# Five of the row turns of a two-layer SSM and MLP step as DMA transposes, with loads, stores and norms rearranged

## The chip, the cores and the metric

The kernel runs on one core of a Trainium2 chip. The metric is the device time of one execution in microseconds (us). Inside a core, TensorE (PE) multiplies matrices, VectorE (DVE), ScalarE (ACT) and GpSimd (POOL) work on elements, and SyncE (SP) only issues DMA transfers; ACT and POOL can issue DMAs too. Each engine runs its own instructions strictly in order, and semaphores join them.

## The reference, cut to what matters

Two kinds of layer alternate twice, on a sequence of 2048 rows with 448 channels, in bf16. The program returns the output and, for a given gradient of the output, the gradients of all nine inputs but `B_x`, which is not used.

```python
def A(q, k, v, shift_k, ssm_k, ssm_D):          # long convolution
    kv = sum(pad(k, 3)[:, t:t+S] * shift_k[:, 3-t] for t in range(4)) * v
    y  = irfft(rfft(pad(kv)) * rfft(pad(ssm_k)))[:S]      # length 2*S
    return q * (y + kv * ssm_D)
def B(x, w1, w2):                               # 448 -> 1792 -> 448
    return silu(x @ w1) @ w2
x = A_q
x = x + A(layernorm(x), ...);  x = x + B(layernorm(x), w1, w2)
x = x + A(layernorm(x), ...);  x = x + B(layernorm(x), w1, w2)
# out = x; and the vector-Jacobian product with grad_out
```

Since k, v and the convolution weights do not depend on x, the convolved rows Y are computed once and serve both A layers.

## The kernel before

The kernel has three stages.

**The prefix** (to about 105 us) transforms the convolution weights and kv with matrix-multiply FFTs and leaves Y in SBUF. At its end the first rows are normalised.

**The main loop**, `Main.run` (L777 and on), goes over four chunks c of 512 rows. A matmul contracts over the partitions, so the normalised rows, which lie with rows on partitions, have to be turned before w1 can be applied: `nT` holds them with channels on partitions, as four blocks of 128 channels (the last two overlap) by 512 rows. The steps are generators, and a hand-written string says in what order PE runs them (`weave`): one letter is one step.

- H is `h = nT x w1` (seven steps of 8 products, L510), with silu on ACT and a transposed store of the activation, `aT`.
- O is the product with w2 (L692, eight steps of 7 matmuls), whose result DVE adds to the rows X.
- G is the gradient through w2 (L510, seven steps), N the gradient through w1 (L738, eight steps of 7 matmuls) with the backward pass of the norms on DVE.
- T is a turn: `transp` (L570 to 578) makes eight 128x128 PE transposes into a PSUM bank, which ACT copies to `nT`; a turn has two such steps, so 16 transposes and two copies.
- J is a step of `Jobs`, the weight gradients, whose blocks are read back from HBM. They start in the last chunk and run on into the suffix.

In chunk c the order on PE is: O of layer 1 (with G for the next stretch and, for the chunks 1 and 2, the turn of the next chunk's `n01` rows among its last steps), N of layer 1 woven with H(c+1, 0), O of layer 0, G, and N of layer 0 woven with H(c+1, 1), between whose first steps the `n1` rows of chunk c+1 are turned. H(c+1, 0) and H(c+1, 1) wait for the turned rows, and every step of H needs all 512 rows.

SP's queue is in order too. `store` (L563 to 569) writes each half of an activation or gradient to HBM turned: two DMA transposes SBUF to SBUF (16 and 12 blocks of 128x128) into "turned" buffers, of which there are two, and two plain stores, each behind its transpose's landing. `load_gT` (L762, L763) brings a chunk of grad_out turned from DRAM, as eight DMA transposes of three blocks or one. The `nT` tiles and gT share two buffers.

PE's order is that of the program text. The order on the other engines' queues is made by a planner from its own estimates of when each instruction is due; `issue_after` binds one instruction behind another.

**The suffix**, `_ssm_suffix`, turns the gradient of Y into those of k, v and the convolution weights by FFTs and inverse FFTs, with Jobs woven between. `Jobs.load` (L965 to 981) fetches one block of 512 KB on SP; `load_n3`, `n1` and `go2` fetch the other operands. `spec_load` reads the spectra of the prefix back on POOL. `fin_w2` and `fin_w1` copy results out; `flush` turns w1's. The last seven w2 blocks (f = 7 to 13) come at the very end.

`_ln_steps` (L255 to 281) normalises: batch statistics on DVE, the power on POOL, one DVE instruction for `-mean*rstd` (`ln_nmr`, L273), and one for `x*rstd + nmr` (L278).

Of the kernel before, what the change touches and what calls it, by code (L numbers as in the profile page):

```python
# [10 lines left out]
FP32 = mybir.dt.float32  # L11
BF16 = mybir.dt.bfloat16
ACT = mybir.ActivationFunctionType
ALU = mybir.AluOpType
# [3 lines left out]
P = 128  # L18
S = 2048
D = 448  # L20
# [87 lines left out]

def _copy(nc, eng, out, in_):
    if eng is nc.scalar:  # L110
        nc.scalar.copy(out, in_)
    else:
        eng.tensor_copy(out, in_)


class K:
# [86 lines left out]
def _fft_stage1(k, n2, rhs, A1, psum, m=None, eng=None):  # L203
    nc = k.nc
    ps = psum.tile([P, 2, 512], FP32, name="ps_s1", **k.pt["s1"])
    for c in range(2):
        nc.tensor.matmul(ps[:, c, :D], lhsT=k.M1sb[:, n2 if m is None else m, c, :], rhs=rhs, start=True, stop=True)  # L207
    _copy(nc, eng or nc.scalar, A1[:, :, :, n2, :].rearrange("p dh c ds -> p c dh ds"), ps[:, :, :D].rearrange("p c (dh ds) -> p c dh ds", ds=4))


def _fft_stage2(k, Zt, psum, consume, chunks=range(NCI)):
# [41 lines left out]
def _ln_steps(k, pool, c, src, si, n_g, groups=((0, 4),), pin=False, eng=None, behind=None, store=()):  # L253
    nc = k.nc
    for lo, hi in groups:  # L255
        n = hi - lo
        st = pool.tile([P, 4, 6], FP32, name="ln_st", tag="ln_st", bufs=1)
        mv = pool.tile([P, 4, 2], FP32, name="ln_mv", tag="ln_mv", bufs=2)
        for tl in range(lo, hi):
            with ExitStack() as es:  # L260
                if behind:
                    es.enter_context(k.tc.issue_after(behind[tl].ins))
                i = nc.vector.bn_stats(out=st[:, tl, :], in_=src(tl))
            if pin:
# [7 lines left out]
        nmr = pool.tile([P, 4], FP32, name="ln_nmr", tag="ln_nmr", bufs=2)  # L272
        nc.vector.scalar_tensor_tensor(out=nmr[:, lo:hi], in0=mv[:, lo:hi, 0], scalar=-1.0, in1=r[:, lo:hi], op0=ALU.mult, op1=ALU.mult)  # L273
        for tl in range(lo, hi):
            if eng is nc.scalar:
                nc.scalar.activation(n_g[:, tl, :], src(tl), ACT.Identity, bias=nmr[:, tl:tl + 1], scale=r[:, tl:tl + 1])
            else:
                k.ln_last = nc.vector.tensor_scalar(out=n_g[:, tl, :], in0=src(tl), scalar1=r[:, tl:tl + 1], scalar2=nmr[:, tl:tl + 1], op0=ALU.mult, op1=ALU.add)  # L278
# [256 lines left out]
class Main:  # L535
# [221 lines left out]
    def load_gT(self, c, gT):  # L757
        nc = self.nc
        src = _pm(self.k.grad_out[0])
        for tl in range(4):  # L760
            ts = slice(tl * P, (tl + 1) * P)
            nc.sync.dma_start_transpose(out=gT[:, 0:3, ts], in_=src[:, 4 * c + tl, 0:384])  # L762
            nc.sync.dma_start_transpose(out=gT[:, 3:4, ts], in_=src[:, 4 * c + tl, 320:448])  # L763

    def T(self, src, dst):
        for h in range(2):
            self.transp(src, dst, h)
            yield
# [12 lines left out]
    def run(self, es):  # L781
# [52 lines left out]
        for c in range(4):  # L834
# [7 lines left out]
            steps("OOOO", O=o)  # L842
            if c < 3:
                self.fwd0b(c + 1)
            if c == 0:
                weave("O" * 4, O=o)
            else:
                if c == 1:
                    gh2, g = gh21, g21
                else:  # L850
                    gh2 = []
                    g = self.G(gT, gh2)
                if c == 1:
# [18 lines left out]
            if c < 3:  # L872
                r = []
                if c == 0:
                    weave("NTNTNHNNHHNNHHNHH", N=n, T=self.T(self.n0[1][1], nT), H=self.H(c + 1, 0, nT, r, (10, 11)))
                else:
                    weave("NHNNHHNNHHNNHHN", N=n, H=self.H(c + 1, 0, nT, r))
                gb = gb_load(c + 1)
                aT, dT1 = r
                weave("OOOOOOTOTO", O=self.O(c + 1, 0, aT), T=tg)  # L880
                self.fwd1(c + 1, [self.chain] * 4)
                g = self.G(gT, gh1, dT0)
                if c:
                    gT = self.nT()
                    self.load_gT(c + 1, gT)
                    weave("G" * 7, G=g)
                else:
                    weave("G" * 7, G=g)
# [30 lines left out]
class Jobs:  # L919
# [48 lines left out]
    def load(self, key, ft):  # L968
        k, nc = self.k, self.nc
        i = self.n_ld  # L970
        self.n_ld += 1
        if self.pool is None and i % 2 and i > 3:
            st = _hd(k, [P, NT, P], "dstat")
        else:
            st = k.dp3.tile([P, NT, P], BF16, name="dstat", tag="dstat", bufs=3)
        src = k.OP_d[key]
        with ExitStack() as es:
            if self.last_ld is not None:
                es.enter_context(k.tc.issue_after(self.last_ld.ins))
            self.last_ld = nc.sync.dma_start(out=st[:], in_=src[:, ft, :, :])  # L980
        return st
# [46 lines left out]
    def steps(self):  # L1028
# [39 lines left out]
    def fin_w2(self, ft, ps):  # L1068
        nc, k = self.nc, self.k
        o = self.out()  # L1070
        if ft == NF - 1:
            nc.scalar.copy(o[:, 0:256], ps[:, 0:256])
            nc.vector.tensor_copy(o[:, 256:D], ps[:, 256:D])
        else:
            nc.scalar.copy(o[:], ps[:, :D])
# [59 lines left out]
def _ssm_suffix(k):  # L1135
# [9 lines left out]
    with ExitStack() as es:  # L1145
# [6 lines left out]
        B1k = A1[:].rearrange("p a c n s -> p (a c n s)").rearrange("p (q d) -> p q d", d=D)  # L1152
        for n2 in range(16):
            k.M1sb = k.m1h[n2 // 8]
            _fft_stage1(k, n2, gY[:, n2, :], A1, psum, n2 % 8)
            jobs.run(1)
        with ExitStack() as e1:
            p1 = e1.enter_context(tc.tile_pool(name="sspec2", bufs=1, reuse_waits="tile"))
# [7 lines left out]
            def spec_load(cp):  # L1166
                lo, hi = cp * 2048, (cp + 1) * 2048
                kk = (kk0 if cp == 0 else kk1 if cp == 1 else sp.tile([P, 2, 2048], BF16, name="kk_c", tag="kk0") if cp % 2 == 0
                      else p1.tile([P, 2, 2048], BF16, name="kk_d", tag="kk1"))
                nc.gpsimd.dma_start(out=kk[:, 0, :], in_=k.SPEC_d["K"][:, lo:hi])  # L1170
                i = nc.gpsimd.dma_start(out=kk[:, 1, :], in_=k.SPEC_d["KV"][:, lo:hi])
                if cp == 2:
                    with tc.issue_after(i.ins):
                        _load_minv(k, nc.gpsimd)
                return kk

            kks = [spec_load(0)]
            for g in range(7):
                pt = psum.tile([P, 16, P], BF16, name="ps_tr", **mm)
                for i in range(16):  # L1180
                    nc.tensor.transpose(pt[:, i, :], A1f[:, 16 * g + i, :], k.ident[:])  # L1181
                if g % 2:
                    nc.scalar.copy(Zf[g], pt[:].rearrange("p a b -> p (a b)"))
# [83 lines left out]
        for dc in range(ND):  # L1267
            gK = p2.tile([DC, S], BF16, name="gK", tag="gK", bufs=3)
            gKv = gK[:].rearrange("p (n1 n2) -> p n1 n2", n2=16)
            for g in range(2):  # L1270
# [82 lines left out]
```

## Time and profile before

| | us |
|---|---|
| median of three runs | 727.19 |
| the three runs | 723.72, 729.2, 727.19 |
| the profiled execution | 728.88 |
| its span, first to last instruction | 727.1 |
| PE busy | 693.8 (95%) |
| DVE busy | 490.2 (67%) |
| ACT busy | 441.3 (61%) |
| POOL busy | 124.9 (17%) |
| SP queue's DMAs (q1), share of 16 DMA engines | 61.5% |
| mean TensorE clock granted | 0.990 |

The main loop takes about 103 to 503 us of the span, 92 us a chunk. In views of the trace, a line names the engine, the source line, the operation and its tiles (`out<-in`), and after a bar or in brackets the idle time ahead of it with what ended it. A timeline line starts with start and duration in us; `x8` means that eight equal neighbours are joined. `SPq` is SP's queue of DMA issues: the duration is that of the issue, not of the transfer. PEclk is the clock granted to TensorE, 1.00 being full speed. A DMA landing is counted from its issue.

### The profile page before, as it was taken

How to read it: one execution, taken by the hardware profiler on the slowest of the kernel's cores; microseconds unless marked ns; L12 is line 12 of the kernel's file. 1: busy time of each engine (PE TensorE's matmuls, PEld its weight loads, DVE VectorE, ACT ScalarE, POOL GpSimd, SP SyncE). 2: the span in 40 equal slices, each digit the busy share in tenths (PEclk: the TensorE clock that was granted, in tenths of full speed). 3: DMA queues.
4: the chain of work that ended last, by engine and by line, in shares of the span. 5: the costliest groups of instructions: out<-in, count | busy, mean ns of one | idle time of the engine just before them, and what ended most of it. 6: DMA issues, size and time to landing. Idle time of an engine off the chain costs nothing.

```text
span 727.1 us, 12759 instructions
## 1 busy us (share of the span) xinstructions
PE 693.8 (95%) x4976; PEld 379.6 (52%) x4976; DVE 490.2 (67%) x1150; ACT 441.3 (61%) x577; POOL 124.9 (17%) x213
## 2 busy tenths in 40 slices
PE   6998989899999999999999999999699999999898
PEld 4876644334444444444444444545366666656554
DVE  5789866668886758975488525635058778859780
ACT  4877978585877869587786783224555555454200
POOL 1134310101020100111002000001112233243230
PEclk9999999999999999999999999999989999999999
DMA  9949997569978999599885995299997798689871
GB/s 323 284 130 299 355 318 183 138 156 254 219 143 233 272 232 222 135 195 268 205 204 122 220 306 203 59 240 224 372 341 279 267 347 316 210 297 350 304 231 39
DMA packets 196093, 172.59 MB, mean 237 GB/s; under 512 B 142946, under 2 KB 174050, under 8 KB 194880
## 3 DMA queue, kind: packets, MB, share of 16 engines
q1 hardware_dynamic: 181568, 116.87, 61.5%
q0 software_dynamic: 14000, 54.90, 21.1%
q8 instruction: 39, 0.64, 0.4%
q14 instruction: 22, 0.18, 0.1%
q10 hardware_dynamic: 464, 0.00, 0.0%
HBM read 73.25 MB, written 60.10 MB: 183 GB/s over the span
## 4 chain that ended last, share of the span: by engine, by line
PE 77%; DMA 7%; DVE 5%; ACT 5%; issue 4%; POOL 1%; SPq 0%; POOLq 0%; ACTq 0%; DVEq 0%
PE ps_d L986 18%; PE ps_n L738 12%; PE ps_g L510 11%; PE ps_h L510 11%; PE ps_o L692 8%; PE ps_v L228 2%; PE ps_d L1021 2%; PE ps_v L227 2%; DMA dstat<-a_d 2%; PE ps_cv L383 2%; DMA out_dram<-gK 2%; DMA KB<-Z 1%; PE ps_t L577 1%; PE ps_s L207 1%; PE ps_tr L1181 1%
## 5 line engine op out<-in xcount | busy, mean ns | idle before, releaser
L986 PEld LDWEIGHTS <-dstat 128*128 128x128 bf16 x800 | 76.0, 98 | 72.7 <-DMA dstat<-a_d 6.4
L510 PE MATMUL ps_h<-nT,w1sb 128*128 128x512 bf16 (+1 forms) x448 | 98.1, 382 | 2.6 <-ACT dT L675 1.9
L738 PE MATMUL ps_n<-w1T,ghT 128*128 128x448 bf16 x448 | 92.5, 353 | 0.5 <-DVE ghT L862 0.5
L692 PE MATMUL ps_o<-w2sb,aT 128*128 128x448 bf16 x448 | 88.5, 352 | 0.0
L510 PE MATMUL ps_g<-nT,w2T 128*128 128x512 bf16 (+1 forms) x392 | 83.8, 383 | 0.1
L720 ACT CAST ghT<-ps_g 128x512 bf16<-128x512 f32 (+1 forms) x74 | 54.1, 759 | 43.4 <-PE ps_g L510 43.3
L670 ACT ACTIVATE aT<-ps_h 128x512 bf16<-128x512 f32 (+1 forms) x82 | 60.0, 760 | 29.2 <-PE ps_h L510 28.8
L510 PEld LDWEIGHTS <-w1sb 128*128 128x128 bf16 (+1 forms) x448 | 35.8, 97 | 60.6 <-issue 27.0
L738 PEld LDWEIGHTS <-ghT 128*128 128x128 bf16 x448 | 43.2, 98 | 42.2 <-DVE ghT L722 1.4
L692 PEld LDWEIGHTS <-aT 128*128 128x128 bf16 x448 | 43.5, 98 | 40.1
L510 PEld LDWEIGHTS <-w2T 128*128 128x128 bf16 (+1 forms) x448 | 35.5, 97 | 55.3 <-issue 21.3
L911 DVE SCALAR_TENSOR_TENSOR lb_v<-lb_u,n 128x448 bf16<-128x448 bf16 x48 | 30.0, 624 | 45.2 <-ACT lb_u L742 44.6
L271 POOL TENSOR_TENSOR rstd<-ln_ve,mhalf 128x2 f32<-128x2 f32 (+2 forms) x27 | 22.3, 826 | 199.2 <-DVE ln_ve L269 199.2
L685 ACT ACTIVATE dT<-dT 128x1024 bf16<-128x1024 bf16 (+1 forms) x64 | 55.0, 936 | 0.1
L986 PE MATMUL ps_d<-n1m,dstat 128*128 128x448 bf16 x224 | 48.6, 352 | 0.0
L986 PE MATMUL ps_d<-n3m,dstat 128*128 128x448 bf16 x224 | 48.6, 352 | 0.0
L227 PE MATMUL ps_v<-Gsb,pa 128*128 128x128 bf16 x336 | 43.9, 222 | 2.2 <-DVE pa L467 2.2
L228 PE MATMUL ps_v<-Gsb,pb 128*128 128x128 bf16 x336 | 43.3, 223 | 1.5 <-DVE pb L468 1.3
L675 ACT CAST dT<-ps_h 128x1024 bf16<-128x1024 f32 (+1 forms) x50 | 42.9, 874 | 0.0
L986 PE MATMUL ps_d<-X,dstat 128*128 128x448 bf16 x176 | 38.9, 365 | 3.2 <-DMA dstat<-a_d 3.2
L742 ACT ACTIVATE lb_u<-ps_n,rstd 128x448 bf16<-128x448 f32 x32 | 20.7, 648 | 34.2 <-PE ps_n L738 26.3
L986 PE MATMUL ps_d<-go,dstat 128*128 128x448 bf16 x176 | 37.2, 353 | 3.9 <-DMA dstat<-a_d 2.3
(208 smaller groups left out, 1192.3 us busy)
## 6 DMA issues: line engine op xcount, KB each, us to landing
dstat<-g_d SPq DMA_DIRECT2D x28, 512.0 KB, 4.5
dstat<-a_d SPq DMA_DIRECT2D x26, 512.0 KB, 6.1
a_d<-turned SPq DMA_DIRECT2D x16, 512.0 KB, 4.1
g_d<-turned SPq DMA_DIRECT2D x16, 512.0 KB, 3.4
a_d<-turned SPq DMA_DIRECT2D x16, 384.0 KB, 3.1
g_d<-turned SPq DMA_DIRECT2D x16, 384.0 KB, 3.3
N_d<-n POOLq DMA_DIRECT2D x10, 448.0 KB, 4.2
spec_K<-Z POOLq DMA_DIRECT2D x7, 512.0 KB, 6.6
```

Source lines behind the costliest of these rows:

```text
L227: nc.tensor.matmul(pv[:, i, :], lhsT=pa[:, i * P:(i + 1) * P], rhs=k.Gsb[:, ga, :], start=True, stop=False)
L228: nc.tensor.matmul(pv[:, i, :], lhsT=pb[:, i * P:(i + 1) * P], rhs=k.Gsb[:, gb, :], start=False, stop=True)
L271: k.ln_pow = nc.gpsimd.tensor_tensor(out=r[:, lo:hi], in0=ve[:, 0:n], in1=k.mhalf[:, 0:n], op=ALU.pow)
L510: nc.tensor.matmul(ps(u, u + 1)[:, 0, :], lhsT=wT[h, b, ft * P:(ft + 1) * P], rhs=rhs[h, b, :], start=start, stop=stop)
L670: self.last_silu = nc.scalar.activation(aT[hh][:, o:o + hi - lo, :], ps(lo, hi), ACT.Silu)
L675: nc.scalar.copy(self.dpart(dT, 2 * fp + lo, 2 * fp + hi), ps(lo, hi))
L685: self.nc.scalar.activation(d[:, o:o + n, :], d[:, o:o + n, :], ACT.Derivative_silu)
L692: nc.tensor.matmul(po[:, :D], lhsT=aT[ft // 7][:, ft % 7, tl * P:(tl + 1) * P], rhs=self.w2sb[:, ft, :], start=(ft == 0), stop=(ft == NF - 1))
L720: nc.scalar.copy(g, ps(lo, hi))
L738: nc.tensor.matmul(pn[:, :D], lhsT=gh[ft // 7][:, ft % 7, tl * P:(tl + 1) * P], rhs=self.w1T[:, ft, :], start=(ft == 0), stop=(ft == NF - 1))
L911: nc.vector.scalar_tensor_tensor(out=v[:], in0=u0, scalar=-1.0 / D, in1=n_t, op0=ALU.mult, op1=ALU.mult, accum_out=cp[:, 1:2])
L986: self.nc.tensor.matmul(ps[:, :D], lhsT=st[:, t, :], rhs=mov[:, t, :], start=(first and t == 0), stop=(last and t == NT - 1))
```

## The change

1. Norms: on DVE the mean and the reciprocal deviation are used directly, `(x - mean)*rstd`, and `ln_nmr` goes.
2. Five turns, of the n1 rows of chunks 1, 2 and 3 and of the n01 rows of chunks 2 and 3, become `turn_dma`: eight DMA transposes SBUF to SBUF on SP, in the shapes of `load_gT`. They are called T1 (n1, in the loop's pass c = 0), T2 and T3 (n01 and n1, c = 1), T4 and T5 (n01 and n1, c = 2) here. The weave strings lose their T steps; in the N type five steps of N now precede the first of H, where it was four, with the two T steps between. The load of gT moves behind the turn on SP.
3. `Jobs.load` sends the loads numbered 3, 4 and 5 by POOL.
4. The first two spectrum loads go by ACT's queue, behind a named copy, and the gK rows are stored by ACT's queue.
5. In the last w2 blocks the two movers change places, so that X comes ahead of go2, and the last block is made in two column pieces, each copied by ACT and stored on SP.

```diff
+        if eng is nc.scalar:
+            nmr = pool.tile([P, 4], FP32, name="ln_nmr", tag="ln_nmr", bufs=1)
...
-                k.ln_last = nc.vector.tensor_scalar(out=n_g[:, tl, :], in0=src(tl), scalar1=r[:, tl:tl + 1], scalar2=nmr[:, tl:tl + 1], op0=ALU.mult, op1=ALU.add)
+                k.ln_last = nc.vector.tensor_scalar(out=n_g[:, tl, :], in0=src(tl), scalar1=mv[:, tl, 0:1], scalar2=r[:, tl:tl + 1], op0=ALU.subtract, op1=ALU.mult)
...
+    def turn_dma(self, src, dst):
+        nc = self.nc
+        for tl in range(4):
+            ts = slice(tl * P, (tl + 1) * P)
+            nc.sync.dma_start_transpose(out=dst[:, 0:3, ts], in_=src[:, tl, 0:384])
+            nc.sync.dma_start_transpose(out=dst[:, 3:4, ts], in_=src[:, tl, 320:448])
...
+            if c in (1, 2):
+                self.turn_dma(self.n0[c + 1][1], nT)
...
-                    weave("OGGOGGOTOT", O=o, G=g, T=self.T(self.n0[c + 1][1], nT))
+                    weave("OGGOGGOO", O=o, G=g)
                 elif c < 3:
-                    weave("OGOGGOGGGGTOT", O=o, G=g, T=self.T(self.n0[c + 1][1], nT))
+                    weave("OGOGGOGGGGO", O=o, G=g)
...
-                g = self.G(gT, gh1, dT0)
+                nT = self.nT()
+                self.turn_dma(self.n1[1], nT)
+                weave("G" * 7, G=self.G(gT, gh1, dT0))
                 if c:
                     gT = self.nT()
                     self.load_gT(c + 1, gT)
-                    weave("G" * 7, G=g)
...
-                nT = self.nT()
-                weave("NNTNTNHNNHHNNHHHH", N=n, T=self.T(self.n1[1], nT), H=self.H(c + 1, 1, nT, r, (10, 11)))
+                weave("NNNNNHNHNHNHHHH", N=n, H=self.H(c + 1, 1, nT, r, (10, 11)))
...
+        if i in (3, 4, 5):
+            nc.gpsimd.dma_start(out=st[:], in_=src[:, ft, :, :])
+            return st
...
-        for f in range(7, 14):
-            yield from self.group((f,), keys, (self.go2, g2), self.fin_w2)
+        for f in range(7, 13):
+            yield from self.group((f,), keys[::-1], (g2, self.go2), self.fin_w2)
+        yield from self.last_block(keys[::-1], (g2, self.go2))
+
+    def last_block(self, keys, movs):
...
+        for lo, hi in ((0, 320), (320, D)):
+            ps = self.bank(None)
...
+            nc.scalar.copy(o[:, lo:hi], ps[:, lo:hi])
+            nc.sync.dma_start(out=k.outs[8][ft * P:(ft + 1) * P, lo:hi], in_=o[:, lo:hi])
...
-            kks = [spec_load(0)]
+            kks = [spec_load(0, first_copy)]
...
-            kks.append(spec_load(1))
+            kks.append(spec_load(1, turned))
...
-            nc.gpsimd.dma_start(out=out5v[:, dc, :], in_=gK[:])
+            nc.scalar.dma_start(out=out5v[:, dc, :], in_=gK[:])
```

More of the change, by code (lines that the diff above doesn't have):

```diff
@@ L110, in _copy @@
     if eng is nc.scalar:
-        nc.scalar.copy(out, in_)
-    else:
-        eng.tensor_copy(out, in_)
+        return nc.scalar.copy(out, in_)
+    return eng.tensor_copy(out, in_)
 class K:
@@ L207, in _fft_stage1 @@
         nc.tensor.matmul(ps[:, c, :D], lhsT=k.M1sb[:, n2 if m is None else m, c, :], rhs=rhs, start=True, stop=True)
-    _copy(nc, eng or nc.scalar, A1[:, :, :, n2, :].rearrange("p dh c ds -> p c dh ds"), ps[:, :, :D].rearrange("p c (dh ds) -> p c dh ds", ds=4))
+    return _copy(nc, eng or nc.scalar, A1[:, :, :, n2, :].rearrange("p dh c ds -> p c dh ds"), ps[:, :, :D].rearrange("p c (dh ds) -> p c dh ds", ds=4))
 def _fft_stage2(k, Zt, psum, consume, chunks=range(NCI)):
@@ L271, in _ln_steps @@
         k.ln_pow = nc.gpsimd.tensor_tensor(out=r[:, lo:hi], in0=ve[:, 0:n], in1=k.mhalf[:, 0:n], op=ALU.pow)
-        nmr = pool.tile([P, 4], FP32, name="ln_nmr", tag="ln_nmr", bufs=2)
-        nc.vector.scalar_tensor_tensor(out=nmr[:, lo:hi], in0=mv[:, lo:hi, 0], scalar=-1.0, in1=r[:, lo:hi], op0=ALU.mult, op1=ALU.mult)
+        if eng is nc.scalar:
+            nmr = pool.tile([P, 4], FP32, name="ln_nmr", tag="ln_nmr", bufs=1)
+            nc.vector.scalar_tensor_tensor(out=nmr[:, lo:hi], in0=mv[:, lo:hi, 0], scalar=-1.0, in1=r[:, lo:hi], op0=ALU.mult, op1=ALU.mult)
         for tl in range(lo, hi):
@@ L885, in run @@
                     self.load_gT(c + 1, gT)
-                    weave("G" * 7, G=g)
-                else:
-                    weave("G" * 7, G=g)
                 self.slope(dT1, self.last_copy)
@@ L1040, in steps @@
         yield from self.group((12, 13), wkeys, movs, self.fin_w1)
-        for f in range(7, 14):
-            yield from self.group((f,), keys, (self.go2, g2), self.fin_w2)
+        for f in range(7, 13):
+            yield from self.group((f,), keys[::-1], (g2, self.go2), self.fin_w2)
+        yield from self.last_block(keys[::-1], (g2, self.go2))
+    def last_block(self, keys, movs):
+        nc, k = self.nc, self.k
+        ft = NF - 1
+        o = self.out()
+        st = [self.load(key, ft) for key in keys]
+        for lo, hi in ((0, 320), (320, D)):
+            ps = self.bank(None)
+            for i in range(2):
+                mov = movs[i]()
+                for t in range(NT):
+                    nc.tensor.matmul(ps[:, lo:hi], lhsT=st[i][:, t, :], rhs=mov[:, t, lo:hi], start=(i == 0 and t == 0), stop=(i == 1 and t == NT - 1))
+                    if t % 4 == 3:
+                        yield 1
+            nc.scalar.copy(o[:, lo:hi], ps[:, lo:hi])
+            nc.sync.dma_start(out=k.outs[8][ft * P:(ft + 1) * P, lo:hi], in_=o[:, lo:hi])
         self.flush()
@@ L1070, in fin_w2 @@
         o = self.out()
[L1071 to L1075, printed above, removed]
+        nc.scalar.copy(o[:], ps[:, :D])
         self.flush()
@@ L1154, in _ssm_suffix @@
             k.M1sb = k.m1h[n2 // 8]
-            _fft_stage1(k, n2, gY[:, n2, :], A1, psum, n2 % 8)
+            i = _fft_stage1(k, n2, gY[:, n2, :], A1, psum, n2 % 8)
+            if n2 == 13:
+                first_copy = i
             jobs.run(1)
@@ L1164, in _ssm_suffix, with spec_load @@
             A1f = A1[:].rearrange("p a c n s -> p a (c n s)")
-            def spec_load(cp):
+            def spec_load(cp, behind=None):
                 lo, hi = cp * 2048, (cp + 1) * 2048
@@ L1169, in spec_load @@
                       else p1.tile([P, 2, 2048], BF16, name="kk_d", tag="kk1"))
+                if behind is not None:
+                    with tc.issue_after(behind.ins):
+                        for j, nm in enumerate(("K", "KV")):
+                            nc.scalar.dma_start(out=kk[:, j, :], in_=k.SPEC_d[nm][:, lo:hi])
+                    return kk
                 nc.gpsimd.dma_start(out=kk[:, 0, :], in_=k.SPEC_d["K"][:, lo:hi])
@@ L1182, in _ssm_suffix @@
                 if g % 2:
-                    nc.scalar.copy(Zf[g], pt[:].rearrange("p a b -> p (a b)"))
+                    turned = nc.scalar.copy(Zf[g], pt[:].rearrange("p a b -> p (a b)"))
                 else:
```

## The prediction

> **What bounds the kernel now.** I read the busy shares first, then the main loop by chunk, then PE's waits, then SP's queue at the places where the turns go. Times are microseconds (us) from the start of the span.
>
> ```profile
> PE 693.8 (95%) x4976; PEld 379.6 (52%) x4976; DVE 490.2 (67%) x1150; ACT 441.3 (61%) x577; POOL 124.9 (17%) x213
> ```
> ```profile
> core 0: us, PE busy (x) PEld busy (x) DVE busy (x) ACT busy (x) POOL busy (x), PEclk, DMA share, GB/s
> 175.00:267.00 92.00, 91.00 (x496) 42.02 (x494) 67.66 (x192) 70.57 (x94) 9.38 (x13) 1.00 0.94 218
> 267.00:359.00 92.00, 91.17 (x495) 41.98 (x493) 64.06 (x184) 69.72 (x94) 9.38 (x13) 1.00 0.88 210
> ```
> TensorE (PE) is the bound, and in the main loop it idles for under 1 us of 92: its instruction order is written by hand, and everything in it stands behind an instruction that waits, so whatever makes PE wait there lengthens the kernel one for one, and whatever leaves PE shortens it. ACT and DVE have 21 to 28 us of slack per chunk. The PE waits that can still be gained lie behind the loop:
>
> ```profile
> PE ps_d L986 <- DMA dstat<-a_d: 5.5, 2, 3.2
> PE ps_t L777 <- DVE n L278: 1.9, 1, 1.9
> PE ps_d L986 <- DMA go<-in_grad_out_dram: 1.5, 1, 1.5
> PE ps_sk L1288 <- DMA out_dram<-gK: 1.5, 1, 1.5
> ```
> (total, times, longest.) And what the longest wait leaves behind, by stretches (PEclk is the third number from the end):
> ```profile
> 513.00:517.00 4.00, 4.00 (x22) 2.08 (x23) 0.00 (x0) 2.27 (x3) 0.55 (x1) 1.00 0.97 383
> 525.30:527.00 1.70, 1.61 (x5) 0.72 (x6) 0.00 (x0) 0.00 (x0) 0.00 (x0) 0.50 1.00 393
> 527.00:529.00 2.00, 2.00 (x7) 0.72 (x6) 0.00 (x0) 0.91 (x1) 0.00 (x0) 0.50 1.03 412
> 529.00:531.00 2.00, 2.00 (x18) 1.86 (x17) 0.00 (x0) 0.00 (x0) 0.00 (x0) 0.50 1.09 436
> ```
> After PE waited 3.21 us (until 525.39) the granted clock was 0.50 for 5.7 us, which costs 2.85 us more. After 1.92 us (until 141.69) it was 0.57 over 142 to 146, about 1.9 us. After 2.34 us (until 512.93) it stayed 1.00. A wait of two to three us thus costs itself plus 0, 1.9 or 2.9.
>
> **Loads and stores behind the loop: gain 11.5.** The waits at 512.93 and 525.39 are for a_d blocks loaded on SP behind other loads (one was issued at 509.74 and landed 15.6 later). Three of these loads go to POOL, whose queue is 17% busy, and the n3m load is issued about 14 us sooner; the first spectrum loads move off POOL to later points of ACT's queue, out of the stretch 510 to 525 (DMA share 0.97 to 1.09); the blocks they serve are read at 547 or later. Taken: 2.34 + 3.21 + 2.85 = 8.4; bounds 4 (the bytes are the same, so one wait may stay) and 8.4. In the last w2 blocks X goes ahead of go2, whose load was issued at 662.13 and landed after 11.5: the wait of 1.5 goes (bounds 0 and 1.5). The gK stores move from POOL to ACT; ACT waited 7.43 for one to land before it could write gK (677.26), and PE 1.46 behind it: 1.5 (bounds 0 and 1.5). The last block becomes 64 matmuls of 320 and 128 columns in place of 32 of 448, and ends with a copy of 128 columns instead of 256 (0.37 to about 0.25): 0.1.
>
> **Norms: gain 0.7.** 27 DVE instructions of 0.16 go; DVE is not the bound, so only where PE waits for DVE: the 1.92 before 141.69. Its chain loses two or three of them, 0.3 to 0.5, and perhaps a little clock; bounds 0 and 1.9. Prefix reordering on POOL and ACT: 1 us either way, taken as 0.
>
> **The five turns, PE and ACT side.** Each turn is 16 PE transposes; two rows around 219.53 and 221.41 show what eight cost PE:
>
> ```profile
> 216.88 2.81 PE L738 MATMUL ps_n<-w1T,ghT 128*128 128x448 bf16 x14
> 219.53 0.61 PE L577 MATMUL ps_t<-ident,n 128*128 128x128 bf16 x8
> 219.98 1.49 PE L738 MATMUL ps_n<-w1T,ghT 128*128 128x448 bf16 x7
> 221.41 0.61 PE L577 MATMUL ps_t<-ident,n 128*128 128x128 bf16 x8
> 221.85 1.49 PE L738 MATMUL ps_n<-w1T,ghT 128*128 128x448 bf16 x7
> 223.18 1.89 PE L510 MATMUL ps_h<-nT,w1sb 128*128 128x512 bf16 x8
> ```
> 219.53 to 219.98 and 221.41 to 221.85: 0.89 per turn, 4.4 in all. The ten ACT copies (1.008 each) were hidden.
>
> **The turns on SP.** A turn becomes 8 DMA transposes in SP's in-order queue, and H, the next user, needs all of them: every product runs over all 512 rows. The nearest rows are the loads of gT, with the same shapes but from DRAM:
>
> ```profile
> 290.31 1.26 SPq L762 DMA_TRANSPOSE nT<-in_grad_out_dram  x1
> 291.60 1.23 SPq L763 DMA_TRANSPOSE nT<-in_grad_out_dram  x1
> 292.88 1.26 SPq L762 DMA_TRANSPOSE nT<-in_grad_out_dram  x1
> ```
> They follow each other 1.29 apart, whether of three blocks or one, and land 2.5 (median) after the issue. The SBUF-to-SBUF transposes of this kernel are larger: 1.27 at the shortest for 16 blocks, 1.46 for 12. The same floor in both kinds says that a fixed cost per instruction rules, so I take 7 x 1.29 + 2.5 = 11.5 per turn. Bounds: 0.40 apart (a plain store takes 0.36 on SP), 5.3 per turn; and 1.81 apart (the series from 105.58 to 116.42), 15.2.
>
> Where the five stand, by SP's order in the changed program (need = when PE would reach H without the transposes and, for the N type, with one more N step of 1.32 ahead of H; that step is work moved, so a turn costs its idle time less 0.89):
> - T1, chunk 0 (N type, turned between steps of N): behind the g_d stores of the first half, so from 219.96 + 0.36 = 220.3 (its rows were ready at 216.8, four us before SP comes to it). Done 231.8; need 223.18 - 0.89 + 1.32 = 223.6. Idle 8.2, net **+7.3**.
> - T2, chunk 1 (O type, turned among the last steps of O): behind the a_d store at 251.29, from 251.65 (rows ready 247.5). Done 263.2; need 260.25 - 0.89 = 259.4. Idle 3.8, net **+2.9**.
> - T3, chunk 1 (N type): half of it behind the 16-block transpose of ghT (299.96, about 1.8), half behind the 12-block one (1.5): 299.96 + 1.8 + 4 x 1.29 + 1.5 + 3 x 1.29 + 2.5 = 314.8; need 310.39 - 0.89 + 1.32 = 310.8. Idle 4.0, net **+3.1**.
> - T4, chunk 2 (O type): behind the store at 339.31, from 339.7; done 351.2; need 352.74 - 0.89 - 0.31 (a wait for the copy, which goes) = 351.5. Just hidden, net **-1.2**.
> - T5, chunk 2 (N type): as T3, from 392.46: done 407.3; need 402.89 + 0.43 = 403.3. Idle 4.0, net **+3.1**.
>
> Sum +15.2. Behind T3 and T5 the next chunk's eight gT loads start some 10 us later on SP, and the stores of ghT behind them too; gT is read only 20 us later, and SP's own rows sum to 46 to 54 us of a 92 us chunk, so I take 0. Nothing is late on ACT or DVE; they are pushed with PE.
>
> **The clock after the new waits.** T1 surely pays the 2.9; T2, T3 and T5 are as long as the wait that paid 2.9, but I give them the mean of the three cases seen, (0 + 1.9 + 2.9)/3 = 1.6 each. Sum +7.7; bounds 2.9 and 11.6. The Trainium skill, "TensorE: Matmul & The Clock Gate", Part 1 (What's actually happening), says that an idle window of about 3.4 us halves the clock, that the window runs free, and that a like window of work restores it. That fits the rows at 525 and the lucky one at 512.93; by it all four waits are likelier to pay, and the sum would be 3.9 higher.
>
> **Sum against the profiled run.** 728.88 (span 727.1 and 1.8 around it) - 11.5 - 0.7 + 15.2 + 7.7 = 739.6. That run lies 1.7 above the median of 727.19, so I predict **738** beside that median. One per cent, 7.3 us, is about what a measurement of this kernel can tell from no change: the runs shown spread over 5.5.
>
> **Rivals.**
> - Small SBUF transposes are cheap to issue (ends faster). For: no small SBUF-source transpose is in the trace, and the 16- and 12-block means (1.80, 1.44) would extrapolate to 0.63 and 0.45. Against: the common floor of 1.25. At 0.40 apart T1 is done at 225.6 (idle 2.0, net +1.1, clock up to +1.9), the others are hidden (-0.9, -0.9, -0.9, -1.2): -12.2 - 0.9 gives 715.8, beside the median 714; at 0.63 and 0.45, 716. It decides at T2 below 0.74 apart: (259.4 - 251.65 - 2.5)/7. "Advanced Engine Details and Errata", X-Bar Transpose (TRN2), in the Trainium skill says that transpose DMAs are as fast as regular ones; the gT rows, 1.23 against 0.36, do not bear that out for the issue. Another of its pages, "VectorE: DVE Perf Modes", The three transpose paths, gives 1309 ns for a 128x128 block by DMA and advises TensorE where PSUM will do, which speaks against this change. Chance 0.22.
> - The waits come, but the clock mostly holds, or a little less is lost per turn: 726 to 731, no change. For: 512.93. Chance 0.13.
> - The queue backs up: issues 1.81 apart among the stores, and T4 no longer hidden. Each of four waits grows 3.7, T4's idle is 3.4: +20, up to 758. For: DMA share 0.88 to 0.94 here. Against: SP's slack. Chance 0.14.
> - The change doesn't do what it says in my favour: SP's planner-given place proves harmless and all five are hidden: -12.2 - 4.7 = 712, beside the median 710. Chance 0.05.
>
> **Numbers.** Forecast 738 (own range 731 to 746), chance 0.46. Faster by over 1% (below 720): most of the cheap issue and the last, 0.27. Within 1%: the second rival, and the forecast's low end up to 734.5, 0.22. Slower 0.51. The range 716 to 757 takes in the bounds of the issue time and leaves out the last rival and the tails.
>
> **What would show it.** PE waiting for nT at H after each turn: about 8, 4, 4, 0, 4, each with PEclk near 0.5 behind it; rows of nT<-n on SP about 1.25 each; no wait near 512 and 525; none before the first go2 block. If nT<-n takes 0.4 to 0.6, or H does not wait in chunk 1, the forecast is wrong and the kernel is faster.

## The result, and the profile after

The changed kernel takes 761.57 us (median of four runs, 757.82 to 766.84) against 725.46 for the kernel before, a ratio of 1.050 with a 95% interval of 1.046 to 1.054. It is slower, as forecast, but by 36 us and not by 11, and outside the range. The profiled execution took 763.06, 34.2 more than the one before.

The same views as before, now of the changed kernel. The busy shares, and the longest of PE's waits (total, times, longest):

```profile
PE 697.3 (92%) x4928; PEld 376.8 (49%) x4928; DVE 487.3 (64%) x1122; ACT 432.2 (57%) x568; POOL 123.0 (16%) x208
...
PE ps_h L510 <- DMA nT<-n: 24.6, 5, 8.0
PE ps_d L996 <- DMA dstat<-a_d: 9.6, 1, 9.6
...
PE ps_h L510 <- issue: 3.3, 1, 3.3
```

PE is busy for longer though 80 transposes left it (the last block adds 32 matmuls), and it waits 27.9 us for turned rows and 9.6 for a weight block. The wait of 3.3 that the view puts down to "issue" is one for turned rows too: it ended at 328.30, and the last three-block transpose of T3 had landed at 328.21. Each first H behind a turn, in PE's timeline (start, duration, and in brackets the idle time before it and what ended it):

```profile
230.39 3.65 PE L510 MATMUL ps_h<-nT,w1sb 128*128 128x512 bf16 x8 [7.99 <-DMA nT<-n]
...
271.49 3.60 PE L510 MATMUL ps_h<-nT,w1sb 128*128 128x512 bf16 x8 [3.09 <-DMA nT<-n]
328.30 1.23 PE L510 MATMUL ps_h<-nT,w1sb 128*128 128x512 bf16 x3 [3.34 <-issue]
330.35 2.31 PE L510 MATMUL ps_h<-nT,w1sb 128*128 128x512 bf16 x5 [0.83 <-DMA nT<-n]
...
379.10 3.57 PE L510 MATMUL ps_h<-nT,w1sb 128*128 128x512 bf16 x8 [7.09 <-DMA nT<-n]
437.25 3.57 PE L510 MATMUL ps_h<-nT,w1sb 128*128 128x512 bf16 x8 [5.59 <-DMA nT<-n]
```

The eight matmuls after each wait take 3.6 us where they took 1.89. The stretches around the first wait show why (the third number from the end is the granted clock): 0.50 for six us, then 1.00 again.

```profile
222.00:230.40 8.40, 0.41 (x4) 0.04 (x2) 3.10 (x10) 1.14 (x1) 0.77 (x2) 0.75 0.35 84
230.40:232.00 1.60, 1.60 (x4) 0.38 (x5) 0.00 (x0) 0.00 (x0) 0.00 (x0) 0.50 0.23 47
232.00:234.00 2.00, 2.00 (x6) 0.73 (x5) 0.00 (x0) 0.00 (x0) 0.00 (x0) 0.50 1.14 211
234.00:236.00 2.00, 2.00 (x7) 0.73 (x5) 0.00 (x0) 1.93 (x2) 0.00 (x0) 0.50 1.14 209
236.00:238.00 2.00, 2.00 (x10) 0.75 (x10) 0.62 (x3) 0.72 (x2) 0.00 (x0) 0.90 1.01 324
```

The turns' instructions, from the view of the tile nT (min, median and max of one issue in ns, then the landing in us):

```profile
L769 SPq DMA_TRANSPOSE nT<-n x20: 1199/1253/2595, 220.3 to 433.4; - x20
L770 SPq DMA_TRANSPOSE nT<-n x20: 1226/1232/1943, 221.5 to 434.6; - x20
...
DMA to landing us min/median/max: 2.3/2.6/8.0
```

The landing line counts the gT loads too, which write the same tile; the 40 transposes of the turns alone land 2.4 us (median) after their issue.

1.25 us of SP's time for three blocks, 1.23 for one: the floor that the gT rows suggested holds for SBUF sources too.

Where the 34.2 us lie can be read from when PE starts the same work in both executions: the O steps that follow each H, and the first FFT step of the suffix.

| PE starts | before | after | difference | growth | forecast of the growth |
|---|---|---|---|---|---|
| O(1, 0) | 193.39 | 192.11 | -1.3 | -1.3 (prefix and norms) | -0.7 |
| O(1, 1), after T1 | 240.76 | 249.63 | +8.9 | +10.2 | +10.2 |
| O(2, 0), after T2 | 280.95 | 295.07 | +14.1 | +5.2 | +4.5 |
| O(2, 1), after T3 | 327.97 | 348.44 | +20.5 | +6.4 | +4.7 |
| O(3, 0), after T4 | 373.44 | 401.79 | +28.4 | +7.9 | -1.2 |
| O(3, 1), after T5 | 420.48 | 455.44 | +35.0 | +6.6 | +4.7 |
| first FFT of the suffix | 503.24 | 538.20 | +35.0 | 0 | 0 |
| end of the span | 727.1 | 761.3 | +34.2 | -0.8 | -11.5 |

The turns cost 36.3 and not 22.9; the suffix gained 0.8 and not 11.5. A turn's growth less its wait, with the 0.89 of PE work (and for T4 the copy's 0.31) added back, is what the clock took: 3.1, 3.0, 3.1, 2.0 and 1.9, or 13.1. The granted clock was 0.50 for about six us behind the first three waits and about four behind T4 and T5, which fits.

### The profile page after: what moved, and what is told of

The parts are those of the page before. It is cut to its first block, busy times and chain, and to the rows that moved or that the text cites. A ratio compares the mean times of both kernels' runs of the same rounds, so it can differ in the third digit from the quotient of the medians.

```text
span 761.3 us, 12719 instructions
## 1 busy us (share of the span) xinstructions
PE 697.3 (92%) x4928; PEld 376.8 (49%) x4928; DVE 487.3 (64%) x1122; ACT 432.2 (57%) x568; POOL 123.0 (16%) x208
## 3 DMA queue, kind: packets, MB, share of 16 engines
q0 software_dynamic: 13344, 52.54, 20.5%
## 4 chain that ended last, share of the span: by engine, by line
PE 67%; DVE 11%; DMA 7%; ACT 6%; issue 5%; POOL 2%; SPq 1%; DVEq 0%; POOLq 0%; ACTq 0%
PE ps_d L996 18%; PE ps_h L510 11%; PE ps_n L738 9%; PE ps_g L510 7%; PE ps_o L692 5%; PE ps_d L1031 2%; DMA turned<-ghT 2%; PE ps_v L227 2%; PE ps_v L226 2%; DVE ln_st L262 2%; POOL rstd L270 2%; PE ps_cv L383 2%; DMA nT<-n 2%; ACT dT L685 2%; DMA KB<-Z 1%
## 5 line engine op out<-in xcount | busy, mean ns | idle before, releaser
L510 PE MATMUL ps_h<-nT,w1sb 128*128 128x512 bf16 (+1 forms) x448 | 106.2, 402 | 30.5 <-DMA nT<-n 24.6
L996 PEld LDWEIGHTS <-dstat 128*128 128x128 bf16 x768 | 72.8, 98 | 71.7 <-DMA dstat<-a_d 10.0
L738 PE MATMUL ps_n<-w1T,ghT 128*128 128x448 bf16 x448 | 96.1, 364 | 2.1 <-DVE X L696 2.1
L510 PEld LDWEIGHTS <-w2T 128*128 128x128 bf16 (+1 forms) x448 | 35.3, 97 | 54.9 <-issue 20.5
L270 POOL TENSOR_TENSOR rstd<-ln_ve,mhalf 128x2 f32<-128x2 f32 (+2 forms) x27 | 22.9, 849 | 211.7 <-DVE ln_ve L268 211.7
L996 PE MATMUL ps_d<-X,dstat 128*128 128x448 bf16 x160 | 35.5, 362 | 9.6 <-DMA dstat<-a_d 9.6
L227 PEld LDWEIGHTS <-pb 128*128 128x128 bf16 x336 | 32.6, 98 | 7.9 <-DVE pb L468 5.0
```

The lines of the kernel that those rows point to most:

```text
L227: nc.tensor.matmul(pv[:, i, :], lhsT=pb[:, i * P:(i + 1) * P], rhs=k.Gsb[:, gb, :], start=False, stop=True)
L510: nc.tensor.matmul(ps(u, u + 1)[:, 0, :], lhsT=wT[h, b, ft * P:(ft + 1) * P], rhs=rhs[h, b, :], start=start, stop=stop)
L738: nc.tensor.matmul(pn[:, :D], lhsT=gh[ft // 7][:, ft % 7, tl * P:(tl + 1) * P], rhs=self.w1T[:, ft, :], start=(ft == 0), stop=(ft == NF - 1))
L996: self.nc.tensor.matmul(ps[:, :D], lhsT=st[:, t, :], rhs=mov[:, t, :], start=(first and t == 0), stop=(last and t == NT - 1))
```

## The experiments

Times are medians, with the ratio to the kernel before in the same session and its interval; ratios are compared, since the kernel before itself gave 724.1 to 729.2 in them.

**Turns undone, and turns alone.** First the changed kernel with the turns back on PE, all else kept:

```diff
-            if c in (1, 2):
-                self.turn_dma(self.n0[c + 1][1], nT)
...
+                    weave("OGGOGGOTOT", O=o, G=g, T=self.T(self.n0[c + 1][1], nT))
...
+                weave("NNTNTNHNNHHNNHHHH", N=n, T=self.T(self.n1[1], nT), H=self.H(c + 1, 1, nT, r, (10, 11)))
```

> The changed kernel with its five turns back on PE (and the gT load where it was); norms, loads, stores and last block stay changed. Theory: by the starts of the O and FFT steps the turns account for +36.3 us of the profiled difference (waits for nT 28.0, clock 13.2, PE work saved 4.8), and the rest of the change for about -2; so 725.5 - 2 = about 723 to 726, no difference from before that can be told, with the 9.6 us wait for an a_d block still there behind the loop. Rival: that late block is itself a consequence of SP being backed up by the turns; then it goes too, with the clock behind it, and the gain first forecast for the loads appears: 711 to 714.

Measured: 723.3, ratio 0.997 (0.993 to 1.001), and still a wait of 6.0 us for an a_d block at 524.96. The theory's number; the rival falls, since the late block comes without the turns too. Then the reverse edit on the kernel before:

> The kernel before with only the five turns made DMA transposes (and the gT load behind them). Theory: the whole +36 of the loop appears: 725.5 + 36 = 761 to 763, with PE waits for nT near 8, 3, 4, 7 and 5.5 us. Rival: some of these waits come from the norms or the other rearrangements; then it stays below 755.

Measured: 758.0, ratio 1.042 (1.035 to 1.049), with waits for nT of 7.3, 2.7, 4.1, 9.1 and 4.9. The turns by themselves cost 30 us by the ratio, 33 by the medians. In the profiled execution the first FFT step starts 35.3 us later than before, as in the changed kernel (35.0). But the suffix is 4.4 us shorter than before, where the changed kernel's is 0.8 shorter: the waits for a_d fall from 5.5 to 2.3 here, and in the changed kernel one of 9.6 came, 3.5 more than without the turns.

**The clock.** PE is given matmuls to do while it waits:

```diff
+    def fill(self, n):
+        ps = self.k.psum.tile([P, 512], FP32, name="ps_fill", tag="tr", bufs=1)
+        for j in range(n):
+            self.nc.tensor.matmul(ps[:, 0:D], lhsT=self.w1sb[:, 0, 0:P], rhs=self.w2sb[:, j % NF, :], start=j == 0, stop=j == n - 1)
+        yield
...
-                    weave("NHNNHHNNHHNNHHN", N=n, H=self.H(c + 1, 0, nT, r))
+                    weave("NFHNNHHNNHHNNHHN", N=n, F=self.fill((0, 14, 36)[c]), H=self.H(c + 1, 0, nT, r))
...
-                weave("NNNNNHNHNHNHHHH", N=n, H=self.H(c + 1, 1, nT, r, (10, 11)))
+                weave("NNNNNFHNHNHNHHHH", N=n, F=self.fill((40, 20, 28)[c]), H=self.H(c + 1, 1, nT, r, (10, 11)))
```

> The changed kernel with extra matmuls that nobody reads put on PE right ahead of the five H that wait: 40, 14, 20, 36 and 28 of 448 columns (7.5, 2.6, 3.8, 6.8 and 5.3 us at 0.189 each), a little less than the waits. It does more work than the reference asks, and the result is the same. Theory: the time lost behind the waits is the clock alone, so the clock stays at 1.00, the 13.2 us go, and the time is 748, though PE executes 26 us more. Should the sooner PE only wait longer for SP, part of it is lost again: up to 755. Rival: the slower matmuls behind the waits have another cause (DMA or memory traffic); then 761 or more.

Measured: 756.8, ratio 1.042 (1.035 to 1.049), above the theory's 748 to 755. In the stretches where T1's wait was and behind T4's, of which 4.4 us are left:

```profile
230.00:232.00 2.00, 1.46 (x8) 0.53 (x7) 0.00 (x0) 0.00 (x0) 0.00 (x0) 1.00 0.58 109
232.00:234.00 2.00, 2.00 (x12) 1.01 (x11) 0.00 (x0) 1.82 (x3) 0.00 (x0) 1.00 1.14 211
...
376.00:379.00 3.00, 3.00 (x9) 0.81 (x8) 0.00 (x0) 0.00 (x0) 0.00 (x0) 0.50 0.76 142
```

With PE kept busy the clock stays at 1.00 (twelve matmuls in two us, where it was six); behind the 4.4 us that T4 still waits it is 0.50. From O to O the stretches with T1, T2, T3 and T5 are 2.5, 2.2, 2.3 and 2.1 us shorter: 9.1 in all. So the slow matmuls were the clock, and its cause was the idle time. But the gain does not stay: in the stretch of T4 PE waits 4.4 more on top of its 6.8 of filler, which makes it 3.8 longer, and from O(3, 1) to the suffix it is 6.3 longer, with a wait of 3.29 at 482.67 for the first weight blocks, whose loads had come to their turn on SP no sooner. What PE saves it then waits for SP: the first FFT step starts at 538.61, 0.4 us later than in the changed kernel. The 9.1 us by which the whole profiled execution is shorter lie in the suffix, where the wait for the a_d block is 1.4 instead of 9.6.

Whether a wait of two us costs clock is luck here. In all runs with the changed norms PE waits for DVE at the same place of the first chunk. Here in the changed kernel, where the clock stayed at 1.00:

```profile
169.20 1.49 PE L738 MATMUL ps_n<-w1T,ghT 128*128 128x448 bf16 x7 [2.09 <-DVE X L696]
```

and with the turns undone, where it was 0.53 over 168 to 170:

```profile
168.05 2.73 PE L738 MATMUL ps_n<-w1T,ghT 128*128 128x448 bf16 x7 [2.09 <-DVE X L696]
```

**T4 and the backlog.** T3 alone goes back to PE:

```diff
-                nT = self.nT()
-                self.turn_dma(self.n1[1], nT)
+                if c != 1:
+                    nT = self.nT()
+                    self.turn_dma(self.n1[1], nT)
```

> The changed kernel with only the turn T3 (n1 rows, pass c = 1) back on PE. Theory: T4's 7.1 us wait in pass c = 2, which was forecast at nothing, is the backlog that T3 and the gT load behind it leave on SP; without T3 it falls below 1 us. T3's own 6.4, T4's 7.1 and its clock 2.0 go: 745 to 748. Rival: T4 waits because of its own place behind the a_d stores; then it still waits 5 us or more and the time is 754 to 757.

Measured: 740.5, ratio 1.016 (1.013 to 1.020), some 24 us less than with T3. From O(2, 1) to O(3, 0) it takes 44.1 us, where the changed kernel takes 53.35 and the kernel before 45.5: T4 does not wait at all, and even its forecast of -1.2 is met. That the time is below the theory's 745 to 748 goes with two waits that the theory left as they were: T5's fell from 5.6 to 3.5, the one for the a_d block from 9.6 to 5.9. SP's timeline says how T3 got in its way. In the changed kernel (start, duration of the issue):

```profile
327.13 1.23 SPq L770 DMA_TRANSPOSE nT<-n  x1
328.41 0.58 SPq L567 DMA_DIRECT2D g_d<-turned  x1
329.09 0.51 SPq L569 DMA_DIRECT2D g_d<-turned  x1
329.71 2.07 SPq L762 DMA_TRANSPOSE nT<-in_grad_out_dram  x1
...
340.24 1.23 SPq L763 DMA_TRANSPOSE nT<-in_grad_out_dram  x1
341.57 3.96 SPq L563 DMA_TRANSPOSE turned<-ghT  x2
...
367.26 0.36 SPq L569 DMA_DIRECT2D a_d<-turned  x1
367.72 2.43 SPq L769 DMA_TRANSPOSE nT<-n  x1
```

and with T3 on PE:

```profile
321.65 4.20 SPq L563 DMA_TRANSPOSE turned<-ghT  x2
...
347.81 2.37 SPq L769 DMA_TRANSPOSE nT<-n  x1
```

T3 ends at 328.4, the gT load fills SP until 341.5, and the second half of ghT, the two halves of aT and their stores follow in a row. Each store waits on SP for its transpose to land, and each transpose for one of the two buffers, that is for an earlier store to land: of the 26.2 us from 341.57 to 367.72, 17.3 are issues and 8.8 waits. T4's first transpose goes out at 367.7; the shift of PE up to there is 20.5, and 339.7 + 20.5 would have been 360.2. The 7.5 us that it is late are T4's wait of 7.1.

**The a_d block.** First the three loads back to SP, with the turns as changed:

```diff
-        if i in (3, 4, 5):
-            nc.gpsimd.dma_start(out=st[:], in_=src[:, ft, :, :])
-            return st
```

> The changed kernel with the three a_d loads back on SP instead of POOL, which also puts the n3m load back behind them. Theory: the 9.6 us wait is due to the n3m load, which now stands ahead of the last gradient's transposes on SP; it goes with the clock behind it (2.9), and the two waits of before return (2.3 and 3.2 and the clock 2.9): 761.6 - 12.5 + 8.4 = 757 to 758. Rival: the backlog of SP makes the block late whatever the order: 761 or more.

Measured: 753.3, ratio 1.036 (1.029 to 1.043), 10 us better by the ratios, and better than the theory's 757 to 758. The waits for a_d are 1.3 in all; the two old ones did not come back. Why the edit hurts can be followed in the chain of waits and SP's timeline of the changed kernel. Here is the chain (start, us, what):

```profile
542.28 16.20 DMA turned<-ghT
558.48 0.02 issue
558.50 0.36 SPq L569
558.86 0.04 issue
558.90 5.25 DMA dstat<-a_d
564.15 0.05 issue
564.19 1.68 PE ps_d L996 x4
```

and here what stands before it on SP:

```profile
531.42 0.42 SPq L1091 DMA_DIRECT2D n3m<-N_d  x1
532.92 11.58 SPq L563 DMA_TRANSPOSE turned<-ghT  x2
545.23 0.36 SPq L567 DMA_DIRECT2D g_d<-turned  x1
558.50 0.36 SPq L569 DMA_DIRECT2D g_d<-turned  x1
558.90 1.38 SPq L990 DMA_DIRECT2D dstat<-a_d  x2
```

The n3m load (1.75 MB) is bound behind the last load that went by SP. With three loads gone to POOL that is an older one, and so n3m now starts ahead of the last two transposes of ghT. Those take 11.6 us to issue and one lands after 16.2; the store of g_d waits for it, and the a_d loads stand behind the store. The load itself stands only beside the first of the two, which landed at 545.21; n3m had landed at 542.52, when the second had just gone out. Beside the second are six transfers that POOL issued from 542.02 to 546.09, one of them an a_d load. To test that n3m's place is the cause, the loads stay on POOL, the turns are on PE, and n3m is bound behind the last store:

```diff
-        with k.tc.issue_after(self.last_ld.ins):
+        with k.tc.issue_after(self.main.last_store.ins):
             k.nc.sync.dma_start(out=self.n3[:], in_=_pm(k.N_d[3][:]))
```

> The changed kernel with its turns back on PE and the three a_d loads on POOL as changed, but the n3m load held behind the last g_d store on SP. Theory: that load's place ahead of the last gradient's transposes is the whole cost of the load edit; their landing falls from about 10 to 17 us back to 4 to 7, the 6.0 us wait falls below 2.5, and the time is that of the run with these loads on SP or a little better: 0.980 to 0.990 of the kernel before. Rival: the three loads on POOL are in the way themselves (they share the DMA engines with the transposes): 0.994 to 1.000.

Measured: 719.0, ratio 0.990 (0.985 to 0.995), where the turns undone alone gave 0.997. The longest landing of these transposes falls from 13.0 (turns undone) to 8.0, the wait from 6.0 to 2.2. The last transpose of ghT has landed at 504.40, before POOL's next transfers go out (from 504.47). The rival's 0.994 touches the interval; a later run with n3m in this place and these loads on POOL, the control with short rings below, gave 0.988 to 0.993 and excludes it. So the loads on POOL are harmless once n3m is in its place. The same with the loads on SP:

> The changed kernel with its turns back on PE and the three a_d loads back on SP, so norms, spectrum loads on ACT, gK stores, and the last blocks are what is left of the change. Theory: the 6.0 us wait for an a_d block in the run with only the turns undone comes from the n3m load standing ahead of the last gradient's transposes; it goes with the clock behind it, as it did with the turns in place (-8), and 723.3 becomes 714 to 716: faster than the kernel before by 1.2%. Rival: without the backlog of the turns the blocks on SP are as late as before (2.3 and 3.2 us): 722 to 724.

Measured: 720.4, ratio 0.988 (0.985 to 0.991), as the theory had it by the ratio, if not in us. Both are faster than the kernel before by about 1%, and their intervals overlap: that moving the three loads to POOL gains anything is not shown. What the spectrum loads have to do with it:

```diff
-            kks = [spec_load(0, first_copy)]
+            kks = [spec_load(0)]
...
-            kks.append(spec_load(1, turned))
+            kks.append(spec_load(1))
```

> The changed kernel with its turns back on PE, the three a_d loads on SP, and the first two spectrum loads back on POOL; norms, gK stores and last blocks stay changed. Theory: moving the spectrum loads is what took the 3.2 us wait and its clock away; so both come back, +6: 0.994 to 0.998 of the kernel before, where it was 0.988. Rival: the gain was elsewhere (last blocks, gK stores, norms): 0.986 to 0.990.

Measured: 720.5, ratio 0.994 (0.991 to 0.997). A wait of 3.5 us for an a_d block at 510.62 is there again where it was 2.1. That is the theory's lower edge, but the two intervals touch, so that the spectrum loads are worth some 4 us is likely and not settled.

**Is it the eight instructions?** Each turn as one DMA transpose, with the rows first laid out by DVE:

```diff
+            self.spare, n00 = _hd(k, [P, 2048], "x0c"), _hd(k, [P, 4, D], "n00")
...
     def turn_dma(self, src, dst):
         nc = self.nc
-        for tl in range(4):
-            ts = slice(tl * P, (tl + 1) * P)
-            nc.sync.dma_start_transpose(out=dst[:, 0:3, ts], in_=src[:, tl, 0:384])
-            nc.sync.dma_start_transpose(out=dst[:, 3:4, ts], in_=src[:, tl, 320:448])
+        nb = self.spare[:].rearrange("p (b t f) -> p b t f", b=ND, t=4)
+        nc.vector.tensor_copy(nb[:, 0:3], src[:, :, 0:384].rearrange("p t (b f) -> p b t f", b=3))
+        nc.vector.tensor_copy(nb[:, 3], src[:, :, 320:448])
+        nc.sync.dma_start_transpose(out=dst[:].rearrange("p b (t s) -> p (b t) s", t=4), in_=self.spare[:])
```

> The changed kernel with each of the five turns as one DMA transpose of 16 blocks instead of eight of 3 and 1; DVE first copies the rows into the order of the blocks (two copies, into the tile that held the chunk's A_q). The same bytes are turned through the same queue. Theory: the price of a turn is the fixed 1.25 us per transpose instruction on SP, 10 us of eleven; so the turns land 4 to 5 us after their issue, the waits for nT vanish except 1 to 2 us in the pass c = 0, the clock holds, and of the 36 us some 34 go: 722 to 728, with the a_d block still late behind the loop. Rival: it is the bytes, or SP's queue itself (the stores and their landings); then the waits stay above 3 us and the time above 745.

Measured: 745.6, ratio 1.023 (1.018 to 1.029). The theory does not hold. PE's waits:

```profile
PE ps_o L693 <- DVE X L697: 15.8, 2, 13.6
PE ps_d L997 <- DMA dstat<-a_d: 7.5, 1, 7.5
...
PE ps_h L510 <- DMA nT<-x0c: 2.9, 3, 1.8
```

The waits for nT did go, from 27.9 to 2.9, but a wait for DVE came: the next chunk's load of A_q now goes out only behind a turn that reads the tile (327.42 on SP, where the changed kernel has it at 256.50), DVE stands idle for 17.5 us for it, and PE for 13.6. With the loads on SP as well it was no different:

> The changed kernel with one DMA transpose per turn as in the run before, and the three a_d loads back on SP. Theory: both repairs add up: the turns cost PE nothing (4.4 us less than on PE), and no a_d block is late: 711 to 717, faster than the kernel before by over 1%. Rival: the five transposes on SP and the DVE copies push something else late, so that it is no better than the one with turns on PE: 715 to 725.

Measured: 740.5, ratio 1.015 (1.012 to 1.019): the rival in kind, worse in size, by the same wait (13.0). So the tile had to be its own. With one, and with a control that has the same short rings but its turns on PE (both with n3m behind the store):

```diff
+        nb = self.t([P, ND, 4, P], "nb")
...
-            t1 = self.t([P, 2, D], "a_t1", "pr", 3)[:, 0:hi - lo]
+            t1 = self.t([P, 2, D], "a_t1", "pr", 2)[:, 0:hi - lo]
```

> One DMA transpose of 16 blocks per turn as before, but the rows are copied into a tile of their own instead of the one that holds A_q; the room comes from three small rings of DVE that are one buffer shorter (a_t1/g1, lb_u0, lb_v). The n3m load stands behind the last g_d store. Theory: the 13.6 and 2.2 us waits for X in the other one-transpose run came from the shared tile alone; they go, the nT waits stay at 3 us or less, and the five turns cost PE no more than on PE: 0.984 to 0.992 of the kernel before. Rival: DVE's copies or SP's queue delay the norms also with a free buffer: above 1.000.

> The control for the run beside it: turns on PE, n3m behind the last g_d store, and the same three rings one buffer shorter. Theory: DVE has slack of 25 us per chunk, so the shorter rings cost nothing: 0.985 to 0.993 of the kernel before. Rival: they hold up DVE's chain behind N: above 0.997.

Measured: 732.6, ratio 1.011 (1.007 to 1.015), and for the control 718.0, ratio 0.991 (0.988 to 0.993). The control is as expected; the one-transpose turns are not. They wait, but less:

```profile
PE ps_h L510 <- DMA nT<-nb: 12.1, 5, 5.3
...
L770 SPq DMA_TRANSPOSE nT<-nb x5: 2521/4727/5739, 219.8 to 409.8; - x5
```

The wait for X is gone, and nT costs 12.1 us of waiting instead of 27.9. The rest is not the number of instructions. One issue of 16 blocks takes 2.5 to 5.7 us here, and in front of it in the queue stand the stores and transposes of the gradients; in pass c = 1, T2's rows are laid out at 251.28, but it goes out at 257.62, behind a transpose of ghT that started at 255.59, when a store of a_d had landed (255.53) and freed its buffer. Five turns by DMA are 2% slower than the control (1.011 against 0.991) even in this form.

## Why the prediction was wrong

The sign, the bound and the mechanism of the turns were right. Three terms of the sum were not: that T4 is hidden, the price of the clock, and the gain of the loads.

- **The price of a turn: right.** 1.29 apart and 2.5 to land were taken; the issues took 1.25 and 1.23 and landed after 2.4. The three turns for which SP stood as forecast waited 7.99 (8.2 forecast), 3.09 (3.8) and 4.17 (4.0). That they agree so well is luck in part. H does not need all eight to start: its first three products went off when the last three-block transpose had landed, 1.3 us before the end of the turn at T1 (230.39 against 231.66), and PE had come there 1.2 sooner than forecast. T2's turn began on SP 1.2 sooner than forecast, PE's shift counted, and took 13.4 instead of 11.5. The rows for the larger transposes were misread: the shortest with 16 blocks took 1.32 and the shortest with 12 blocks 1.27, and the means are 2.37 and 1.76; the floor stands all the same. The rival of cheap small transposes falls with the turns' rows. The Trainium skill ("Advanced Engine Details and Errata", X-Bar Transpose (TRN2)) says that transpose DMAs are as fast as regular ones; for the issue on SP the trace does not agree, 1.25 against 0.36 for a plain store.
- **T4 hidden, "I take 0": wrong, by 9.1 us** (7.1 of wait and 2.0 of clock). The step that failed is the one behind T3, that SP's own rows sum to half of a chunk and so absorb the ten us of the gT load. The sum of issue times left out the waits for landings that stand in the queue, of stores for their transposes and of transposes for a buffer; in that chain there was no slack, as the run without T3 shows. T5's wait was 1.6 longer than forecast; its 16-block transpose of ghT took 3.1 on SP where 1.8 was taken.
- **The clock: mis-sized, 7.7 against 13.1** (T4's 2.0 is in both points). All five turns' waits paid, T1 to T3 some 3.0 each. To average in the lucky case of 512.93 was the wrong price for waits of 3 us and more, and 13.1 lies above the upper bound of 11.6 since T4 waited too. The matmuls put into the gaps show it to be idle time that costs. The Trainium skill ("TensorE: Matmul & The Clock Gate", Part 1, What's actually happening) gives an idle window of about 3.4 us that runs free, and as long a time of work to recover. By that rule the waits of 3 us and more were likely to pay, as they did; but the lengths do not agree with the trace. Waits of 3.21 and 1.92 before the change, and of 3.09 and 3.34 after it, are shorter than that window and paid, and the clock came back after four to six us.
- **Loads: wrong in sign, 8.4 forecast.** The step said that n3m goes out "about 14 us sooner" and counted this as part of the gain. The same earlier place put 1.75 MB in front of the last gradient's transposes, and through a store that waits the a_d block came 9.6 us late, with a clock of 0.50 to 0.63 for four us behind it. With n3m behind the last store, 5 to 6 us come back (0.997 to 0.990 and 0.988). Against the whole gain of 11.5 forecast behind the loop, the profiled executions from the first FFT step to the end take 223.8 us before, 223.1 in the changed kernel, 220.3 with the turns undone, and, with the turns undone as well, 216.0 with n3m behind the store and 216.4 with the loads on SP.
- **go2 and gK: right.** The waits of 1.5 each at 673.69 and 678.48 are gone. The 0.1 of the last block is too small to be told.
- **Norms: in the range, but not as argued.** The wait of 1.92 became 1.47 and the clock behind it stayed at 1.00, but PE now waits the 2.09 for DVE at 169.20, which neither the kernel before nor the one with the turns alone has. From the first O step to O(1, 0) it takes 75.1 us before, 73.2 in the changed kernel, where the clock held behind the new wait, and 74.9 with the turns undone, where it did not. So the gain is 1.9 or 0.2, by luck; why the new wait comes was not looked into.
- **The rival of the backed-up queue** had the right engine and place, with a chance of 0.14, but a wrong mechanism (slower issues instead of waits for landings in order), and the top of its range left out that the loads' gain could fall at the same time.

## What to carry to other kernels

When work moves from a saturated engine to an in-order DMA queue, price it by the queue: count the issues, add every wait for a landing that stands in that queue, and ask of each later transfer how late it starts. A gap of 3 us on PE cost about 6 here (3.09 and 3.0, before the change 3.21 and 2.85), because the clock falls with it. For gaps of about two us it was open: behind waits of 2.09, 2.17, 2.31 and 2.34 the clock stayed at 1.00, and behind waits of 2.09, 2.14, 2.16 and 2.33, in other executions, it fell to about 0.50. And a load bound "behind the last load" moves when that last load moves: after such an edit, look at what the big transfer now stands in front of.

## What was not expected of the hardware

The issue time of a DMA transpose is no constant above its floor. At the shortest 16 blocks took 1.32 us on SP, but 9.3 right behind the n3m load (from 532.92, until n3m landed), and 2.5 to 5.7 as the one-transpose turn. The transpose of 12 blocks behind it landed 16.2 us after its issue, beside POOL's transfers, where the median of all the "turned" ones was 4.3. That this is the transfers' sharing of the DMA engines (share 0.95 to 1.22 between 534 and 558) fits the run with n3m moved, which brought the longest landing to 8.0; which resource it is was not measured.
